# Moving a step-of-four layout from what TensorE reads to what it writes, in blockwise causal attention with a channel mix

## The chip, the cores and the metric

The kernel runs on one core of a Trainium2 chip. The metric is the time of one execution on the device in microseconds. The kernel before takes 314.23 us, the median of three runs (314.18 to 315.11); the profiled execution spans 312.8 us, with a mean granted TensorE clock of 0.989 of full speed.

## The reference

Eight batches with eight heads of 576 positions and 64 dimensions go through attention in which a query sees all keys of its own block of 64 positions and of earlier blocks. The heads' outputs, side by side, are the input of a channel mix with two matrix products and a gate.

```python
scores = scale * np.matmul(q, k.transpose(0, 1, 3, 2))        # 8 x 8 x 576 x 576
mask = block_i >= block_j                                      # blocks of 64
scores = np.where(mask, scores, -1000000000.0)
attn = np.exp(scores - np.max(scores, axis=-1, keepdims=True))
attn = attn / (np.sum(attn, axis=-1, keepdims=True) + 1e-09)
x = np.matmul(attn, v)                     # then (batch, position, head*dim): 8 x 576 x 512
...
xk = mu_k * x + (1.0 - mu_k) * x_prev      # x_prev: the position before
xr = mu_r * x + (1.0 - mu_r) * x_prev
k = np.maximum(xk @ w_k, 0.0)              # 512 -> 1024
v = k * k @ w_v                            # 1024 -> 512
out = v / (1.0 + np.exp(-(xr @ w_r)))
```

## The kernel before

The work is written as tasks of engines (PE is TensorE, DVE VectorE, ACT ScalarE, POOL GpSimd); a planner in the program puts them in a fixed order for each engine, and TensorE's order is a list of names (`s` scores, `d` and `e` sums, `v` value products, `k`, `r`, `p` the channel mix). Here are the constants, and the steps of attention that the change touches.

```python
P, D, S, CUT, J = 128, 64, 576, 512, 4
M = CUT // J                    # 128: 512 queries are 128 groups (p) of 4 classes (j)
RINGS = {..., "e": 4, "c": 2, "rd": 3, "s": 2, "mm": 4, ...}     # buffers of each kind; s, mm in PSUM
TURNED = 2                      # batches 0 and 1 are transposed on TensorE, 2 to 7 by DMA
```

In batches 0 and 1 the transposed queries (64 dimensions on partitions, queries along the free axis, bf16) lie in their natural order, query 4p + j at column 4p + j. In batches 2 to 7 they lie class by class, query 4p + j at column 128 j + p. The last 64 of the 576 queries are treated by themselves. The keys of a block of 128 are the stationary operand of a score; the two heads of a pair use the two halves of the array's rows. In the later batches one pair of heads has scores of 512, 384, 256 and 128 columns for the first 512 queries, and some of 64 for the last:

```python
LATER = [
    [(0, 0, 0, M)],                                    # (column, key block, groups from, to)
    [(0, 0, M, WD), (D, 1, 32, M), (448, 1, M, WD)],
    [(0, 2, H2, M), (256, 2, M, WD), (320, 3, 96, M), (448, 3, M, WD)],
]
...
if a < M:
    moving = ask[:, J * a:J * z]                       # L649 on: scores
    dst = PS[:, h, col:col + J * w]
    if b >= TURNED:
        moving = ask[:, 0:CUT].rearrange("d (j p) -> d p j", j=J)[:, a:z]
        dst = dst.rearrange("k (p j) -> k p j", j=J)
    nc.tensor.matmul(dst, keys, moving, start=True, stop=True)     # L657
else:
    nc.tensor.matmul(PS[:, h, col:col + D], keys, ask[:, CUT:S], ...)   # L660
```

So scores stand in natural query order in PSUM; in the later batches the moving operand is read with a hop of 128 elements at each element. ScalarE makes exponentials of 1024 of them at a time (two heads, L679), in fp16; GpSimd zeroes those of the first 64 queries of a block against its second 64 keys (L688):

```python
nc.scalar.activation(tiles["e", b, pr][:, :, i, :], tiles["ps", b, pr, i], AF.Exp, scale=ISQ)
...
nc.gpsimd.memset(tiles["e", b, pr][D:P, :, i, col:col + D], 0.0)
```

The sums and the value products use the array as four column tiles of 32, one for each of four heads, that work side by side (all at L721). The sums take one class at a time, so that the sums of class j land on row j of a head's rows; the value products take 32 of the 64 dimensions at a time:

```python
tiled(PS[:, lo - a:z - a], FOURTH[:, (J - j) % J:(J - j) % J + R],      # sums
      probs(b, 4 * Q + g, kc, lo, z)[:, j::J], g, ...)
...
ps = PS[:, cols]                                                        # values
if a < M:
    ps = ps[:, J * (lo - a):J * (z - a)]
tiled(ps, V[:, kc, 4 * Q + g, x:D:2], probs(b, 4 * Q + g, kc, lo, z), g, ...)
```

VectorE takes the reciprocals of the sums (L772, and L775 for the last 64 queries), spreads each class over all rows of its head with a shuffle, and multiplies:

```python
nc.vector.reciprocal(tiles["c", key][:, 0:z - a], PS[:, 0:z - a])       # L772
...
for j in range(J):
    nc.vector.stream_shuffle(tiles["rd", key][:, J * a + j:J * z:J],    # L781
                             tiles["c", key][:, 0:z - a], [j] * 32)
...
num = num[:, 0:n * J * (z - a)].rearrange("p (s t) -> p s t", s=n)[:, :, lo - first:hi - first]
r = r[:, lo - b * S:hi - b * S]
nc.vector.tensor_tensor(x, num, r.unsqueeze(1).to_broadcast([P, n, hi - lo]), ALU.mult)   # L825
```

For each batch but the first and each half of the heads there are one group of sums (`d`), two value products for the first 512 queries (`v` 0 and 1) and one for the last 64 (`v` 2); the first batch has the same columns in two groups.

Of the kernel before, what the change touches and what calls it, by code (L numbers as in the profile page):

```python
# [20 lines left out]
TURNED = 2  # L21
# [259 lines left out]
def kernel(  # L281
# [24 lines left out]
    M = CUT // J  # L306
    WD = M + D
    JT = S // D
    CH = 512
    CHUNKS = [(0, CH // 2), (CH // 2, CH // 2)] + [  # L310
        (i * CH, CH) for i in range(1, B * S // CH)]
# [303 lines left out]
    def add_score(b, pr, i):  # L615


        sbuf = plan.buf("s")
        tail = i is None
        Q = pr // 2  # L620
        takes, uses = [sbuf], [tiles["qktbuf", b]]
        if tail:
            takes.append(el_buf[b][Q])
            deps = sum([evac[x, b, pr + y] for x in ("qkt", "tail")
                        for y in range(2)], [])
            if b:
                deps.append(ready["l", b - 1, Q])
            mms = [(pr + x, x * D, J, M, WD) for x in range(2)]
        else:
            mms = [(pr,) + p for p in pieces(b)[i]]  # L630
            deps = evac["qkt", b, pr] + (
                evac["tail", b, pr] if any(p[3] == M for p in mms) else [])
            if i == 0:
                tiles["ebuf", b, pr] = plan.buf("e")
                takes.append(tiles["ebuf", b, pr])
            else:
                uses.append(tiles["ebuf", b, pr])

        def fn():
            qkt = tiles["qkt", b]  # L640
            PS = tiles["ps", b, pr, i] = new("s", [P, 2, 512], FP)
            if i == 0:
                tiles["e", b, pr] = new("e", [P, 2, 3, 512], F16)
            for p, col, kc, a, z in mms:
                for h in range(2):
                    rows = slice(h * D, h * D + D)
                    keys, ask = qkt[rows, p, 1], qkt[rows, p, 0]
                    w = z - a
                    keys = keys[:, kc * P:kc * P + P]  # L649
                    if a < M:  # L650
                        moving = ask[:, J * a:J * z]
                        dst = PS[:, h, col:col + J * w]
                        if b >= TURNED:
                            moving = ask[:, 0:CUT].rearrange(
                                "d (j p) -> d p j", j=J)[:, a:z]
                            dst = dst.rearrange("k (p j) -> k p j", j=J)
                        nc.tensor.matmul(dst, keys, moving, start=True,  # L657
                                         stop=True)
                    else:
                        nc.tensor.matmul(PS[:, h, col:col + D], keys,  # L660
                                         ask[:, CUT:S], start=True, stop=True)
        pe = on("PE", 0.06 if tail else 0.215 + 0.02 * i, fn, deps, takes, uses,
                name=f"s{b}t{Q}" if tail else f"s{b}{pr}{i}", mode="rows",
                steps=2 * len(mms))
        if tail:
            def exl():
                nc.scalar.activation(
                    E4s[b % 2][0:D, 4 * Q:4 * Q + 4].rearrange(
                        "p (h a) q -> p h a q" if b < TURNED else
                        "p (a h) q -> p h a q", h=2),  # L670
                    tiles["ps", b, pr, i][0:D, :, 0:2 * D].rearrange(
                        "p h (a q) -> p h a q", q=D), AF.Exp, scale=ISQ)
            ready["l", b, Q] = on("ACT", 0.27, exl, [pe],
                                  uses=[sbuf, el_buf[b][Q]])
            return
        ebuf = tiles["ebuf", b, pr]

        def ex():
            nc.scalar.activation(tiles["e", b, pr][:, :, i, :],  # L679
                                 tiles["ps", b, pr, i], AF.Exp, scale=ISQ)  # L680
        t = on("ACT", 0.905, ex, [pe] + ([ready["x", b, pr, 0]] if i else []),
               uses=[sbuf, ebuf])
        ready["x", b, pr, i] = t

        def zero():
            for col, kc, a, z in pieces(b)[i]:
                if a == kc * 32 and a < M:
                    nc.gpsimd.memset(  # L688
                        tiles["e", b, pr][D:P, :, i, col:col + D], 0.0)
        n = sum(a == kc * 32 and a < M for col, kc, a, z in pieces(b)[i])  # L690
        if n:
            ready["z", b, pr, i] = on("POOL", 0.15 * n, zero, [t], uses=[ebuf])

    def probs(b, head, kc, a, z):


        if kc == J:
            return E4s[b % 2][:, head]
        i, col, a0, z0 = [
            (i, col, a0, z0) for i, piece in enumerate(pieces(b))  # L700
            for col, k0, a0, z0 in piece if k0 == kc and a0 <= a and z <= z0][0]
        pr, h = place(b, head)
        E = tiles["e", b, pr][:, h, i, col:]
        if a == M:
            return E[:, 0:D]
        return E[:, J * (a - a0):J * (z - a0)]

    def add_values(b, Q):

# [14 lines left out]
        def sums(PS, a, z):  # L724
            kcs = [kc for kc in range(J) if kc * 32 < z]
            for j in range(J):
                for kc in kcs:
                    lo = max(a, kc * 32)
                    for g in range(G):
                        tiled(PS[:, lo - a:z - a],  # L730
                              FOURTH[:, (J - j) % J:(J - j) % J + R],
                              probs(b, 4 * Q + g, kc, lo, z)[:, j::J], g,
                              (j, kc) == (0, kcs[0]), (j, kc) == (J - 1, kcs[-1]))
            for kc in range(J + 1) if z == M else ():
                for g in range(G):
                    tiled(PS[:, M:WD], ONES, probs(b, 4 * Q + g, kc, M, WD), g,
                          kc == 0, kc == J)

        def part(PS, xs, a, z):
            V = VOs[b % 2]  # L740
            wide = J * (z - a) if a < M else D
            for n, x in enumerate(xs):
                cols = slice(n * wide, n * wide + wide)
                kcs = [kc for kc in range(J) if kc * 32 < z] + [J] * (a == M)
                for kc in kcs:
                    lo = max(a, kc * 32)
                    for g in range(G):
                        ps = PS[:, cols]
                        if a < M:
                            ps = ps[:, J * (lo - a):J * (z - a)]  # L750
                        tiled(ps, V[:, kc, 4 * Q + g, x:D:2],
                              probs(b, 4 * Q + g, kc, lo, z), g,
                              kc == kcs[0], kc == kcs[-1])

        def group(name, a, z, deps, steps, dur, r_dur, s_dur):
# [11 lines left out]

            def recip():
                tiles["c", key] = new("c", [P, M], FP)
                tiles["rd", key] = new("rd", [P, S], FP)  # L770
                PS = tiles["den", key]
                nc.vector.reciprocal(tiles["c", key][:, 0:z - a],  # L772
                                     PS[:, 0:z - a])
                if z == M:
                    nc.vector.reciprocal(tiles["rd", key][:, CUT:S],  # L775
                                         PS[:, M:WD])
            t = on("DVE", r_dur, recip, [t], takes=[cbuf, rd], uses=[dbuf])

            def spread():
                for j in range(J):  # L780
                    nc.vector.stream_shuffle(  # L781
                        tiles["rd", key][:, J * a + j:J * z:J],
                        tiles["c", key][:, 0:z - a], [j] * 32)
            return rd, on("DVE", s_dur, spread, [t], uses=[cbuf, rd]), key

# [20 lines left out]
        def scale(t, i, xs, a, z, c, first, lo, hi, buf, rd, spr, key):  # L806
# [5 lines left out]
            def norm():  # L812
                x = xt_tile(c)[:, ch, 1 + off:1 + off + hi - lo]
                num, r = tiles["num", b, Q, i], tiles["rd", key]
                n = len(xs)
                if a == M:
                    nc.vector.tensor_tensor(
                        x, num[:, 0:n * D].rearrange("p (s t) -> p s t", s=n),
                        r[:, CUT:S].unsqueeze(1).to_broadcast([P, n, D]),
                        ALU.mult)  # L820
                    return
                num = num[:, 0:n * J * (z - a)].rearrange(
                    "p (s t) -> p s t", s=n)[:, :, lo - first:hi - first]
                r = r[:, lo - b * S:hi - b * S]
                nc.vector.tensor_tensor(  # L825
                    x, num, r.unsqueeze(1).to_broadcast([P, n, hi - lo]),
                    ALU.mult)
            dur = 0.2 if a == M else 0.00105 * (hi - lo) * len(xs) + 0.065
            xb = xtbuf[home]
            n = on("DVE", dur, norm, [t, spr], takes=[xb] if take else [],  # L830
# [294 lines left out]
```

## Time and profile before

| | |
|---|---|
| time, median of 3 | 314.23 us |
| span of the profiled execution | 312.8 us |
| TensorE matmul busy | 294.1 us, 94% |
| VectorE busy | 220.5 us, 71% |
| ScalarE busy | 202.1 us, 65% |
| GpSimd busy | 114.1 us, 36% |
| scores of the first 512 queries (L657) | 272 matmuls, busy 71.2 us |
| exponentials (L679) | 96, mean 1024 ns |
| spreading of reciprocals (L781) | 72 shuffles, busy 42.8 us |
| normalisation (L825) | 60, busy 23.6 us |

A line of a group view names the line, engine and operation, the tiles (out<-in), partitions x elements and type, the count, the busy time and the mean of one instruction, and then the idle time of the engine before them with what ended it. In a timeline each row has the start, the time from the first start to the last end of the merged instructions, and their number (x). [...]In the chain of waits, shares belong to the chain of work that ended last.

### The profile page before, as it was taken

How to read it: one execution, taken by the hardware profiler on the slowest of the kernel's cores; microseconds unless marked ns; L12 is line 12 of the kernel's file. 1: busy time of each engine (PE TensorE's matmuls, PEld its weight loads, DVE VectorE, ACT ScalarE, POOL GpSimd, SP SyncE). 2: the span in 40 equal slices, each digit the busy share in tenths (PEclk: the TensorE clock that was granted, in tenths of full speed). 3: DMA queues.
4: the chain of work that ended last, by engine and by line, in shares of the span. 5: the costliest groups of instructions: out<-in, count | busy, mean ns of one | idle time of the engine just before them, and what ended most of it. 6: DMA issues, size and time to landing. Idle time of an engine off the chain costs nothing.

```text
span 312.8 us, 9964 instructions
## 1 busy us (share of the span) xinstructions
PE 294.1 (94%) x4120; PEld 139.5 (45%) x4120; DVE 220.5 (71%) x477; ACT 202.1 (65%) x313; POOL 114.1 (36%) x265
## 2 busy tenths in 40 slices
PE   1987799999999999899999999999999999999996
PEld 1664566344434345424344334443434354444443
DVE  3789999985198935991678817796587728999232
ACT  3868798868776678259761888538865766065360
POOL 3256559430431444343441574325451333000200
PEclk9998699999999999999999999999999999999999
DMA  7999979999999985893969339985942100020303
GB/s 259 308 262 246 245 229 242 256 227 227 263 200 205 234 195 105 190 256 82 206 131 254 126 68 208 188 234 131 173 85 72 69 2 2 34 103 0 137 0 134
DMA packets 118301, 51.51 MB, mean 165 GB/s; under 512 B 102768, under 2 KB 109168, under 8 KB 118256
## 3 DMA queue, kind: packets, MB, share of 16 engines
q1 hardware_dynamic: 118256, 50.88, 68.0%
q8 instruction: 32, 0.52, 0.7%
q14 instruction: 13, 0.11, 0.1%
HBM read 33.56 MB, written 9.44 MB: 137 GB/s over the span
## 4 chain that ended last, share of the span: by engine, by line
PE 80%; DVE 12%; ACT 4%; issue 2%; DMA 1%; SPq 0%; POOL 0%; DVEq 0%; ACTq 0%
PE t_mm L948 19%; PE t_s L657 17%; PE t_mm L1014 17%; PE t_mm L721 13%; PE t_mm L983 10%; DVE t_rd L781 5%; ACT t_e L679 3%; PE t_s L660 2%; DVE t_xt L825 2%; DMA t_ld<-in_q_dram 1%; PE t_mm L469 1%; DVE t_c L772 1%; DVE t_d L897 1%; DVE t_xk L910 1%; DVE t_rd L775 1%
## 5 line engine op out<-in xcount | busy, mean ns | idle before, releaser
L679 ACT ACTIVATE t_e<-t_s 128x1024 f16<-128x1024 f32 x96 | 95.1, 1024 | 53.6 <-PE t_s L660 26.6
L657 PE MATMUL t_s<-t_qkt 64*128 64x128 bf16 (+3 forms) x272 | 71.2, 588 | 1.5 <-ACT t_e L679 1.4
L948 PE MATMUL t_mm<-t_xk,WK 128*128 128x512 f16 (+1 forms) x320 | 69.1, 359 | 1.9 <-DVE t_xt L825 1.2
L1014 PE MATMUL t_mm<-WV,t_k 128*128 128x512 f16 (+1 forms) x296 | 66.1, 374 | 0.5 <-DVE t_o L1026 0.5
L688 POOL MEMSET t_e<- 64x128 f16 x128 | 24.0, 205 | 91.3 <-ACT t_e L679 89.6
L959 ACT ACTIVATE t_kr<-t_mm 128x512 f32<-128x512 f32 (+1 forms) x80 | 43.7, 560 | 18.5 <-PE t_mm L948 17.5
L948 PEld LDWEIGHTS <-WK 128*128 128x128 f16 x320 | 28.9, 98 | 38.7 <-issue 8.8
L1014 PEld LDWEIGHTS <-t_k 128*128 128x128 f16 x296 | 27.4, 98 | 38.4 <-issue 8.7
L772 DVE RECIPROCAL t_c<-t_mm 128x128 f32<-128x128 f32 (+1 forms) x18 | 15.6, 868 | 40.1 <-PE t_mm L721 40.0
L781 DVE STREAM_SHUFFLE t_rd<-t_c 128x128 f32<-128x128 f32 (+1 forms) x72 | 42.8, 868 | 0.0
L968 POOL TENSOR_TENSOR t_k<-t_kr 128x512 f16<-128x512 f32 (+1 forms) x27 | 26.1, 974 | 31.5 <-ACT t_kr L959 31.4
L983 PE MATMUL t_mm<-WR,t_xr 128*128 128x512 f16 x144 | 35.9, 380 | 0.0
L994 ACT ACTIVATE t_t<-t_mm 128x512 f32<-128x512 f32 x36 | 21.5, 600 | 20.5 <-PE t_mm L983 19.9
L968 DVE TENSOR_TENSOR t_k<-t_kr 128x512 f16<-128x512 f32 (+1 forms) x24 | 17.6, 743 | 23.1 <-ACT t_kr L959 23.1
L1026 DVE SCALAR_TENSOR_TENSOR t_o<-t_t,t_mm 128x512 f32<-128x512 f32 (+1 forms) x37 | 24.9, 681 | 12.5 <-PE t_mm L1014 9.6
L721 PE MATMUL t_mm<-t_e,VO 128*32 128x64 f16 (+4 forms) x1056 | 29.4, 251 | 2.1 <-DVE t_xt L825 1.0
L910 DVE SCALAR_TENSOR_TENSOR t_xk<-t_d,MUK,t_xt 128x512 f16<-128x512 f32 (+1 forms) x40 | 28.8, 747 | 1.7 <-POOL t_d L897 1.6
L910 DVE SCALAR_TENSOR_TENSOR t_xr<-t_d,MUR,t_xt 128x512 f16<-128x512 f32 (+1 forms) x40 | 29.8, 770 | 0.0
L660 PE MATMUL t_s<-t_qkt 64*128 64x64 bf16 x320 | 27.7, 204 | 1.1 <-ACT t_e L679 1.1
L825 DVE TENSOR_TENSOR t_xt<-t_mm,t_rd 128x448 f32<-128x448 f32 (+7 forms) x60 | 23.6, 436 | 4.1 <-PE t_mm L721 3.0
L657 PEld LDWEIGHTS <-t_qkt 64*128 64x128 bf16 x272 | 13.8, 101 | 27.5 <-issue 25.1
L721 PEld LDWEIGHTS <-VO 128*32 128x32 f16 x1184 | 19.4, 98 | 14.5 <-issue 6.5
(60 smaller groups left out, 291.0 us busy)
## 6 DMA issues: line engine op xcount, KB each, us to landing
out_dram<-t_o SPq DMA_DIRECT2D x35, 256.0 KB, 2.2
t_vl<-in_v_dram SPq DMA_DIRECT2D x32, 256.0 KB, 4.9
t_ld<-in_k_dram SPq DMA_DIRECT2D x48, 128.0 KB, 4.0
t_ld<-in_q_dram SPq DMA_DIRECT2D x24, 256.0 KB, 4.2
t_ld<-in_q_dram SPq DMA_DIRECT2D x8, 288.0 KB, 5.5
t_ld<-in_k_dram SPq DMA_DIRECT2D x8, 288.0 KB, 5.1
t_ld<-in_moe_w_k_dram SPq DMA_DIRECT2D x8, 256.0 KB, 5.0
t_ld<-in_moe_w_v_dram SPq DMA_DIRECT2D x8, 256.0 KB, 4.3
```

Source lines behind the costliest of these rows:

```text
L657: nc.tensor.matmul(dst, keys, moving, start=True, stop=True)
L660: nc.tensor.matmul(PS[:, h, col:col + D], keys, ask[:, CUT:S], start=True, stop=True)
L679: nc.scalar.activation(tiles["e", b, pr][:, :, i, :], tiles["ps", b, pr, i], AF.Exp, scale=ISQ)
L721: nc.tensor.matmul(ps[g * R:g * R + R], lhs, e, start=start, stop=stop, tile_position=(0, g * R))
L781: nc.vector.stream_shuffle(tiles["rd", key][:, J * a + j:J * z:J], tiles["c", key][:, 0:z - a], [j] * 32)
L825: nc.vector.tensor_tensor(x, num, r.unsqueeze(1).to_broadcast([P, n, hi - lo]), ALU.mult)
L910: nc.vector.scalar_tensor_tensor(tiles[name, h][:, cc, o:o + w], tiles["d", c, cc][:, 0:w], (MUK1, MUR1)[n][:, cc:cc + 1], xt_tile(c)[:, c ...
L948: nc.tensor.matmul(ps[:, 0:w], WK[:, cc, jc * P:(jc + 1) * P], tiles["xk", h][:, cc, o:o + w], start=(cc == 0), stop=(cc == CCn - 1))
L959: nc.scalar.activation(tiles["kr", c, jc][:, 0:w], tiles["pk", c, jc][:, 0:w], AF.Relu)
L968: (nc.vector if eng == "DVE" else nc.gpsimd).tensor_tensor(K2, KR, KR, ALU.mult)
L983: nc.tensor.matmul(ps, tiles["xr", h][:, cc, o + jt * P:o + (jt + 1) * P], WR[:, cc], start=(cc == 0), stop=(cc == CCn - 1))
L1014: nc.tensor.matmul(ps[:, 0:w], tiles["k2", h][:, jc, off:off + P], WV[:, jc, cols], start=(jc == 0), stop=(jc == JCn - 1))
```

## The change

The classes now stay apart from the scores to the exponentials: within one piece the queries stand class by class, so the scores of the later batches and the sums read and write runs of neighbouring elements. The natural order is restored where the value products write PSUM: they write every fourth column, one class after the other. The reciprocals of a class are kept together too, 129 columns from one class to the next, and the multiplication picks them from four places. In batches 0 and 1, whose queries lie in natural order, the scores now read with a step of four elements. The number of instructions, their order, the buffers and the waits are not touched.

```diff
+    MP = M + 1
@@ scores
-                        moving = ask[:, J * a:J * z]
-                        dst = PS[:, h, col:col + J * w]
-                        if b >= TURNED:
-                            moving = ask[:, 0:CUT].rearrange(
-                                "d (j p) -> d p j", j=J)[:, a:z]
-                            dst = dst.rearrange("k (p j) -> k p j", j=J)
-                        nc.tensor.matmul(dst, keys, moving, start=True,
-                                         stop=True)
+                        nc.tensor.matmul(
+                            PS[:, h, col:col + J * w].rearrange(
+                                "p (j n) -> p j n", j=J), keys,
+                            ask[:, 0:CUT].rearrange(
+                                "d (p j) -> d j p" if b < TURNED else
+                                "d (j p) -> d j p", j=J)[:, :, a:z],
+                            start=True, stop=True)
@@ zeroing
-                        tiles["e", b, pr][D:P, :, i, col:col + D], 0.0)
+                        tiles["e", b, pr][D:P, :, i, col:col + J * (
+                            z - a)].rearrange(
+                            "p h (j n) -> p h j n", j=J)[:, :, :, 0:D // J],
+                        0.0)
@@ exponentials as read by sums and values
-        return E[:, J * (a - a0):J * (z - a0)]
+        return E[:, 0:J * (z0 - a0)].rearrange("p (j n) -> p j n", j=J)[
+            :, :, a - a0:z - a0]
@@ sums
-                              probs(b, 4 * Q + g, kc, lo, z)[:, j::J], g,
+                              probs(b, 4 * Q + g, kc, lo, z)[:, j], g,
@@ values
-                            ps = ps[:, J * (lo - a):J * (z - a)]
+                            ps = ps.rearrange("q (n j) -> q j n", j=J)[
+                                :, :, lo - a:z - a]
@@ reciprocals, shuffles
-                tiles["rd", key] = new("rd", [P, S], FP)
+                tiles["rd", key] = new("rd", [P, J * MP + D], FP)
-                        tiles["rd", key][:, J * a + j:J * z:J],
+                        tiles["rd", key][:, j * MP + a:j * MP + z],
@@ normalisation
+                p0, p1 = (lo - b * S) // J, (hi - b * S) // J
                 num = num[:, 0:n * J * (z - a)].rearrange(
-                    "p (s t) -> p s t", s=n)[:, :, lo - first:hi - first]
-                r = r[:, lo - b * S:hi - b * S]
-                nc.vector.tensor_tensor(
-                    x, num, r.unsqueeze(1).to_broadcast([P, n, hi - lo]),
-                    ALU.mult)
+                    "q (s p j) -> q s p j", s=n, j=J)[:, :, p0 - a:p1 - a]
+                r = r[:, 0:J * MP].rearrange("q (j p) -> q p j", j=J)[:, p0:p1]
+                x = x.rearrange("q s (p j) -> q s p j", j=J)
+                if n == 1:
+                    nc.vector.tensor_tensor(x[:, 0], num[:, 0], r, ALU.mult)
+                else:
+                    nc.vector.tensor_tensor(
+                        x, num, r.unsqueeze(1).to_broadcast(
+                            [P, n, p1 - p0, J]), ALU.mult)
... (the last 64 queries' reciprocals move to the end of the wider tile)
```

More of the change, by code (lines that the diff above doesn't have):

```diff
@@ L774, in recip @@
                 if z == M:
-                    nc.vector.reciprocal(tiles["rd", key][:, CUT:S],
+                    nc.vector.reciprocal(tiles["rd", key][:, J * MP:],
                                          PS[:, M:WD])
@@ L818, in norm @@
                         x, num[:, 0:n * D].rearrange("p (s t) -> p s t", s=n),
-                        r[:, CUT:S].unsqueeze(1).to_broadcast([P, n, D]),
+                        r[:, J * MP:].unsqueeze(1).to_broadcast([P, n, D]),
                         ALU.mult)
                     return
+                p0, p1 = (lo - b * S) // J, (hi - b * S) // J
                 num = num[:, 0:n * J * (z - a)].rearrange(
-                    "p (s t) -> p s t", s=n)[:, :, lo - first:hi - first]
-                r = r[:, lo - b * S:hi - b * S]
-                nc.vector.tensor_tensor(
-                    x, num, r.unsqueeze(1).to_broadcast([P, n, hi - lo]),
-                    ALU.mult)
+                    "q (s p j) -> q s p j", s=n, j=J)[:, :, p0 - a:p1 - a]
[7 more added lines that the diff above has]
+                            [P, n, p1 - p0, J]), ALU.mult)
             dur = 0.2 if a == M else 0.00105 * (hi - lo) * len(xs) + 0.065
```

## The prediction

> **What bounds the kernel now.** I read the page from the top, first for the engine that is never idle and then for the stretch in which that holds.
>
> ```profile
> PE 294.1 (94%) x4120; PEld 139.5 (45%) x4120; DVE 220.5 (71%) x477; ACT 202.1 (65%) x313; POOL 114.1 (36%) x265
> ...
> PE 80%; DVE 12%; ACT 4%; issue 2%; DMA 1%; SPq 0%; POOL 0%; DVEq 0%; ACTq 0%
> PE t_mm L948 19%; PE t_s L657 17%; PE t_mm L1014 17%; PE t_mm L721 13%; PE t_mm L983 10%; DVE t_rd L781 5%; ACT t_e L679 3%; PE t_s L660 2%; DVE t_xt L825 2%; DMA t_ld<-in_q_dram 1%; PE t_mm L469 1%; DVE t_c L772 1%; DVE t_d L897 1%; DVE t_
> ```
>
> TensorE is the bound: 94% busy, 80% of the chain of waits. The three lines that the change touches on TensorE are L657 (scores, 17% of the chain), L721 (sums and value products, 13%) and, on VectorE, L781 (spreading the reciprocals, 5%) and L825 (normalisation, 2%). The windows view, cut where attention's first batches end and where the last one ends, says where TensorE has room:
>
> ```profile
> core 0: us, PE busy (x) PEld busy (x) DVE busy (x) ACT busy (x) POOL busy (x), PEclk, DMA share, GB/s
> 0.00:60.00 60.00, 47.47 (x1138) 32.80 (x1142) 49.88 (x130) 46.03 (x77) 33.30 (x79) 0.94 0.98 258
> 60.00:275.00 215.00, 211.94 (x2823) 90.30 (x2815) 150.10 (x315) 138.32 (x205) 78.60 (x184) 1.00 0.69 154
> 275.00:313.00 38.00, 34.72 (x168) 16.36 (x168) 20.56 (x34) 17.77 (x32) 2.25 (x3) 0.99 0.21 77
> ```
>
> Before 60 us no engine is full, and VectorE (49.9 of 60) is busiest; from 60 to 275 us TensorE has 3 us free of 215, while VectorE is at 70% and ScalarE at 64%; after 275 us there is no attention. What the change saves on TensorE is therefore worth most in the middle stretch.
>
> How long single operations occupy TensorE I read from start to start in its timeline, since the duration of one matmul also holds its latency:
>
> ```profile
> 94.84 1.02 PE L657 MATMUL t_s<-t_qkt 64*128 64x512 bf16 x2
> 95.80 1.36 PE L721 MATMUL t_mm<-t_e,FOURTH 128*32 128x128 f16 x64
> 96.98 0.30 PE L721 MATMUL t_mm<-t_e,ONES 128*32 128x64 f16 x16
> 97.10 0.20 PE L721 MATMUL t_mm<-EL,ONES 128*32 128x64 f16 x4
> 97.24 0.20 PE L660 MATMUL t_s<-t_qkt 64*128 64x64 bf16 x2
> 97.28 0.81 PE L657 MATMUL t_s<-t_qkt 64*128 64x384 bf16 x2
> 97.91 0.21 PE L660 MATMUL t_s<-t_qkt 64*128 64x64 bf16 x2
> 97.96 0.59 PE L657 MATMUL t_s<-t_qkt 64*128 64x256 bf16 x2
> 98.38 0.21 PE L660 MATMUL t_s<-t_qkt 64*128 64x64 bf16 x2
> 98.43 0.38 PE L657 MATMUL t_s<-t_qkt 64*128 64x128 bf16 x2
> 98.63 0.21 PE L660 MATMUL t_s<-t_qkt 64*128 64x64 bf16 x2
> 98.77 0.73 PE L721 MATMUL t_mm<-t_e,VO 128*32 128x512 f16 x16
> 99.43 1.02 PE L657 MATMUL t_s<-t_qkt 64*128 64x512 bf16 x2
> ```
>
> A pair of scores 384 wide holds the engine 97.91 - 97.28 = 0.63 us, 256 wide 0.42, 128 wide 0.20: 1.64 ns a column. The sixteen value matmuls (four column tiles side by side, 512 + 384 + 256 + 128 = 1280 columns) take 99.43 - 98.77 = 0.66 us with a change of mode, and the chain of waits has runs of eight full matmuls of 512 in 1.73 us, 0.42 ns a column. So the scores of these batches run at a quarter of the rate. The 64 sum matmuls (four classes of 320 columns, 1280 in all) take 96.98 - 95.80 = 1.18 us, 0.92 ns a column.
>
> **What the Trainium skill says.** "TensorE: Matmul & The Clock Gate", section "Back-to-back issue gap", gives a warm matmul N/2.4 + 2.5 ns; the trace agrees (0.216 us at 512). "Advanced Engine Details and Errata", section "Memory Cachelines", says that SBUF has lines of 16 bytes and needs two hits on a line for full rate. The trace bears out the penalty: scores that hop 256 bytes at each 2-byte element pay four times. It doesn't quite bear out the "two hits": sums that step 8 bytes, two elements to a line, still run at about half rate. "PSUM — Partial Sum Buffer", section "Specifications (TRN2)", says that PSUM's lines are 8 bytes and that "any non-contiguous AP slows matmuls significantly", without a number; nothing in the kernel before writes PSUM with a step, so no row shows the size. "Vector Engine (DVE) Microarchitecture Reference", section "5.2 Measured stream behaviour on trn2", lists 1.05 ns a column for contiguous words, 1.73 where one source hops at every element, 2.5 for small steps. Here the normalisation is contiguous and has 1.04 ns a column ((613 - 281) / (448 - 128) from the groups by form); the shuffle, which writes with a step of 16 bytes, is far worse, as follows.
>
> ```profile
> 126.22 1.00 DVE L781 STREAM_SHUFFLE t_rd<-t_c 128x128 f32<-128x128 f32 x1
> ...
> 126.85 1.00 DVE L781 STREAM_SHUFFLE t_rd<-t_c 128x128 f32<-128x128 f32 x1
> ```
>
> They start 0.62 us apart; those 64 wide start 0.34 apart (31.52, 31.86, 32.20). The slope is (0.62 - 0.34)/64 = 4.4 ns a column, the fixed part 0.06 us.
>
> **The change, part by part.** Instructions, their order, buffers and waits stay; only patterns change, so each item is a number of columns by a new rate.
>
> Scores, batches 2 to 7 (24 pairs of heads): a pair of heads has 1280 such columns, now 0.84 (1.02 less the 0.18 of latency that the 384 wide row shows) + 0.63 + 0.42 + 0.20 = 2.09 us. They read contiguous runs after the change: 1280 x 0.42 = 0.54 us. Saved: 1.55 x 24 = 37 us.
>
> Scores, batches 0 and 1 (8 pairs): now contiguous, then a step of 8 bytes. Charged with about the rate of the sums, 0.4 ns a column more: 1280 x 8 x 0.4 = +4 us.
>
> Sums (16 groups of 1280 columns): contiguous afterwards. Widths 128 and 96 at 0.42 ns, widths 64 and 32 at the 0.03 us that a set of four takes in the rows with ONES (sixteen from 96.98 to 97.10): 0.056 + 0.042 + 0.03 + 0.03 = 0.16 a class, 0.63 a group against 1.18. Saved: 0.55 x 16 = 9 us.
>
> Value products (16 groups, two of 1280 columns each): 40960 columns, 17 us at 0.42. They will write every fourth fp32 word, so each column has an 8-byte line to itself where now two share one. My estimate from the PSUM page is half the rate: +17 us. This is the doubtful term.
>
> TensorE in all: -37 + 4 - 9 + 17 = -25 us, of which the middle stretch (24 pairs, 12 groups) has -37 - 6.6 + 12.8 = -31, and the first 60 us +4 - 2.2 + 4.3 = +6.
>
> VectorE: shuffles written contiguously, estimated at the 1.04 ns of the normalisation over the same fixed 0.06: 0.20 us instead of 0.62 at 128 wide, 0.13 instead of 0.34 at 64. 56 x 0.42 + 16 x 0.21 = -27 us. The normalisation reads the reciprocals with a hop of 129 words at each element; 16 x 1024 columns x (1.73 - 1.04), the first from the page, is an estimate of +11 us. Net -16 us on an engine that is not the bound, but each group's way from sums to normalised values becomes about 1 us shorter. The zeroing on GpSimd (24 us busy) gets shorter runs; I charge nothing.
>
> From engine time to kernel time: in the middle stretch TensorE would need 181 us, VectorE about 150 - 18 + 8 = 140 and ScalarE 138. No engine overtakes TensorE, but matmuls are in a fixed order with two score buffers, and an exponential takes 1.02 us: where scores follow each other closely TensorE, now held 0.65 us by its own scores, will wait for ScalarE. I take three quarters of the saving, -23 us. In the first 60 us TensorE gains 6 us of work but has 12.5 us idle, and VectorE, the busiest, sheds some 4: zero net. 314.2 - 23 = 291 us.
>
> **Rivals.** First, the step in PSUM costs four times rather than twice, like the hops in SBUF: value products +51 us instead of +17, TensorE +9, and with the shorter VectorE chain 314 to 320 us. For it speaks the fourfold price of hopping reads here; against it, that a PSUM line holds only two words, so at most one word is lost. Second, the step costs nothing: TensorE -42 us, about 281. Third, ScalarE takes over as the bound: score waits on the exponentials eat half of the saving, about 299. For it speaks that ScalarE shows 8 or 9 tenths in a third of the middle slices; against it, its mean of 64%. Fourth, the normalisation at 129 words costs the page's 2.5 ns: VectorE +24 instead of +11, nearly what the shuffles save, and 2 or 3 us on the whole.
>
> **Range and chances.** I give the doubled price 55%, a free step 15%, three or four times 25%, worse 5%. These lie at 291, 281, 302 to 318, and above 325. The range 279 to 316 holds the first two and half of the third. Faster by over 2% (below 307.9) then has 0.79, within 2% 0.12, slower 0.09.
>
> **What would show it.** Scores L657 of 512 columns with a duration near 0.4 instead of 1.02 us and 17% of the chain falling to about 5%; sums near 0.65 us from start to start; value products of sixteen taking about 1.1 us (2.1 under the first rival, 0.55 under the second); shuffles about 0.2 us apart; the normalisation of 448 columns near 0.9 us; the exponentials named as releasers of L657 with tens of microseconds if the third rival holds. A value product above 2 us would make the prediction wrong.

## The result, and the profile after

The changed kernel takes 281.82 us (median of four runs, 279.33 to 283.02) against 314.31: a ratio of 0.8951, 95% interval 0.8888 to 0.9015. That is 33.0 us less (0.1049 x 314.3). It lies within the stated range and below the predicted 291.

First the page of the kernel after: the shares of the engines, and the chain of waits by engine and by line. The lines have moved: L652 is the scores, L725 the sums and value products, L786 the shuffles, L833 and L835 the normalisation; L958, L993 and L1024 are the channel mix.

```profile
PE 265.9 (95%) x4120; PEld 134.8 (48%) x4120; DVE 204.0 (73%) x477; ACT 197.0 (70%) x313; POOL 113.2 (40%) x265
...
PE 82%; DVE 7%; ACT 5%; issue 2%; DMA 2%; POOL 0%; SPq 0%; DVEq 0%
PE t_mm L958 22%; PE t_mm L725 18%; PE t_mm L1024 18%; PE t_mm L993 11%; PE t_s L652 7%; ACT t_e L679 3%; PE t_s L660 3%; DMA t_ld<-in_k_dram 2%; DVE t_xt L833 1%; PE t_mm L470 1%; DVE t_d L907 1%; DVE t_o L1036 1%; DVE t_xk L920 1%; ACT t_
```

TensorE is still the bound, with 28.2 us less of work. The scores have gone from 17% of the chain to 7%, the sums and value products together from 13% to 18%, and the shuffles from 5% to under 1% (1.8 us). The windows view, cut again at the first batches and at the end of attention (now near 250 us), shows the middle stretch as full as before, and shorter:

```profile
0.00:60.00 60.00, 49.29 (x1080) 31.68 (x1082) 44.00 (x130) 44.54 (x74) 34.04 (x78) 0.97 0.95 248
60.00:250.00 190.00, 188.50 (x2907) 89.79 (x2902) 145.96 (x327) 139.74 (x218) 77.11 (x186) 1.00 0.87 182
```

TensorE has 1.5 us free of 190 there. Now TensorE's timeline over one stretch, to be read from start to start:

```profile
82.23 0.39 PE L652 MATMUL t_s<-t_qkt 64*128 64x512 bf16 x2
82.55 0.79 PE L725 MATMUL t_mm<-t_e,FOURTH 128*32 128x128 f16 x64
83.18 0.29 PE L725 MATMUL t_mm<-t_e,ONES 128*32 128x64 f16 x16
...
85.91 1.26 PE L725 MATMUL t_mm<-t_e,VO 128*32 128x512 f16 x16
87.10 0.28 PE L652 MATMUL t_s<-t_qkt 64*128 64x256 bf16 x2
```

A pair of scores 512 wide leaves the engine after 0.32 us, with the change of mode; the 64 sums take 83.18 - 82.55 = 0.63 us instead of 1.18; the sixteen value matmuls 87.10 - 85.91 = 1.19 us instead of 0.66. On VectorE the shuffles and the normalisation, as rows of its timeline:

```profile
84.87 0.30 DVE L786 STREAM_SHUFFLE t_rd<-t_c 128x128 f32<-128x128 f32 x1
...
85.08 0.30 DVE L786 STREAM_SHUFFLE t_rd<-t_c 128x128 f32<-128x128 f32 x1
...
87.22 0.82 DVE L833 TENSOR_TENSOR t_xt<-t_mm,t_rd 128x384 f32<-128x384 f32 x1 [0.51 <-PE t_mm L725]
```

The shuffles start 0.21 us apart instead of 0.62.

Adding up by what each matmul moves the end of TensorE's work onward, over the whole trace: scores of the first 512 queries 62.5 us before and 27.2 after, sums 21.6 and 11.8, value products 25.8 and 43.8. That is -35.3, -9.8 and +18.0, -27.1 in all; the other 1.1 us of the 28.2 lie in lines that the change doesn't touch. By the same account TensorE stood idle for 9.2 us between its first and its last matmul before, and for 5.1 after: the span less its busy time, less the time to the first matmul (6.4 and 7.1 us) and less the 3.1 us after the last.

### The profile page after: what moved, and what is told of

Read it like the earlier page. It is cut to its first block, busy times and chain, and to the rows that moved or that the text cites. A ratio compares the mean times of both kernels' runs of the same rounds, so it can differ in the third digit from the quotient of the medians.

```text
span 281.2 us, 9965 instructions
## 1 busy us (share of the span) xinstructions
PE 265.9 (95%) x4120; PEld 134.8 (48%) x4120; DVE 204.0 (73%) x477; ACT 197.0 (70%) x313; POOL 113.2 (40%) x265
## 4 chain that ended last, share of the span: by engine, by line
PE 82%; DVE 7%; ACT 5%; issue 2%; DMA 2%; POOL 0%; SPq 0%; DVEq 0%
PE t_mm L958 22%; PE t_mm L725 18%; PE t_mm L1024 18%; PE t_mm L993 11%; PE t_s L652 7%; ACT t_e L679 3%; PE t_s L660 3%; DMA t_ld<-in_k_dram 2%; DVE t_xt L833 1%; PE t_mm L470 1%; DVE t_d L907 1%; DVE t_o L1036 1%; DVE t_xk L920 1%; ACT t_qkt L392 1%; PE t_mm L1062 1%
## 5 line engine op out<-in xcount | busy, mean ns | idle before, releaser
L958 PE MATMUL t_mm<-t_xk,WK 128*128 128x512 f16 (+1 forms) x320 | 68.9, 358 | 1.3 <-ACT t_kr L969 0.5
L1024 PE MATMUL t_mm<-WV,t_k 128*128 128x512 f16 (+1 forms) x296 | 66.0, 374 | 0.0
L725 PE MATMUL t_mm<-t_e,VO 128*32 128x64 f16 (+4 forms) x1056 | 47.4, 340 | 0.8 <-issue 0.6
L958 PEld LDWEIGHTS <-WK 128*128 128x128 f16 x320 | 29.2, 98 | 32.0 <-issue 3.7
L1024 PEld LDWEIGHTS <-t_k 128*128 128x128 f16 x296 | 27.4, 98 | 32.3 <-issue 2.9
L978 POOL TENSOR_TENSOR t_k<-t_kr 128x512 f16<-128x512 f32 (+1 forms) x27 | 27.1, 1010 | 29.4 <-ACT t_kr L969 29.2
L833 DVE TENSOR_TENSOR t_xt<-t_mm,t_rd 128x448 f32<-128x448 f32 (+6 forms) x56 | 30.8, 593 | 9.5 <-PE t_mm L725 9.1
L652 PE MATMUL t_s<-t_qkt 64*128 64x128 bf16 (+3 forms) x272 | 35.9, 326 | 1.8 <-ACT t_e L679 1.4
L993 PE MATMUL t_mm<-WR,t_xr 128*128 128x512 f16 x144 | 35.9, 380 | 0.0
L725 PEld LDWEIGHTS <-VO 128*32 128x32 f16 x1184 | 24.0, 112 | 21.2 <-issue 18.3
L1036 DVE SCALAR_TENSOR_TENSOR t_o<-t_t,t_mm 128x512 f32<-128x512 f32 (+1 forms) x37 | 24.3, 666 | 10.9 <-PE t_mm L1024 8.6
L978 DVE TENSOR_TENSOR t_k<-t_kr 128x512 f16<-128x512 f32 (+1 forms) x24 | 16.5, 699 | 18.8 <-ACT t_kr L969 18.7
L920 DVE SCALAR_TENSOR_TENSOR t_xr<-t_d,MUR,t_xt 128x512 f16<-128x512 f32 (+1 forms) x40 | 29.5, 763 | 0.0
L660 PE MATMUL t_s<-t_qkt 64*128 64x64 bf16 x320 | 23.7, 196 | 0.4 <-ACT t_e L679 0.3
L907 POOL TENSOR_TENSOR t_d<-t_xt 128x512 f32<-128x512 f32 (+1 forms) x17 | 16.4, 966 | 14.6 <-DVE t_xt L833 11.3
L993 PEld LDWEIGHTS <-t_xr 128*128 128x128 f16 x144 | 13.4, 98 | 16.2 <-issue 0.5
```

Source lines behind the costliest of these rows:

```text
L652: nc.tensor.matmul(PS[:, h, col:col + J * w].rearrange("p (j n) -> p j n", j=J), keys, ask[:, 0:CUT].rearrange("d (p j) -> d j p" if b < T ...
L725: nc.tensor.matmul(ps[g * R:g * R + R], lhs, e, start=start, stop=stop, tile_position=(0, g * R))
L833: nc.vector.tensor_tensor(x[:, 0], num[:, 0], r, ALU.mult)
L920: nc.vector.scalar_tensor_tensor(tiles[name, h][:, cc, o:o + w], tiles["d", c, cc][:, 0:w], (MUK1, MUR1)[n][:, cc:cc + 1], xt_tile(c)[:, c ...
L958: nc.tensor.matmul(ps[:, 0:w], WK[:, cc, jc * P:(jc + 1) * P], tiles["xk", h][:, cc, o:o + w], start=(cc == 0), stop=(cc == CCn - 1))
L978: (nc.vector if eng == "DVE" else nc.gpsimd).tensor_tensor(K2, KR, KR, ALU.mult)
```

## The experiments

Four of them (x1, x2, x3, x10) make one part of the change alone in the kernel before; x5 joins two parts, and the rest undo or vary a part of the changed kernel. Each ratio is to the kernel before on the same chip, and microseconds gained are what the ratio lacks of 1, times 314.3. "TensorE work" and "TensorE idle" are read from one trace of each kernel, counted as above. The work also moves with the granted clock: x3 leaves TensorE's instructions as they were and has 2.6 us less of it, in a trace with a granted clock of 0.999 against 0.989 before. So differences of 2 or 3 us in that column can't be put down to an edit. The time of x8 is the median of three runs; a fourth, of 273.79 us, was in a slower state.

| kernel | time, us | ratio, 95% interval | TensorE work | TensorE idle |
|---|---|---|---|---|
| before | 314.3 | | 294.1 | 9.2 |
| x1: contiguous scores alone | 286.88 | 0.9095 (0.9056 to 0.9134) | 255.1 | 18.9 |
| x2: step of four in PSUM alone | 326.95 | 1.0367 (1.0318 to 1.0416) | 308.8 | 5.4 |
| x3: VectorE's part alone | 310.27 | 0.9836 (0.9797 to 0.9875) | 291.5 | 6.3 |
| x10: contiguous sums alone | 308.85 | 0.9799 (0.9759 to 0.9839) | 286.6 | 10.9 |
| x5: x1 and x3 together | 276.09 | 0.8770 (0.8742 to 0.8799) | 254.8 | 11.1 |
| changed kernel | 281.82 | 0.8951 (0.8888 to 0.9015) | 265.9 | 5.1 |
| x6: changed, VectorE's part undone | 286.32 | 0.9094 (0.9080 to 0.9107) | 266.4 | 8.3 |
| x7: changed, classes 128 apart | 280.28 | 0.8900 (0.8885 to 0.8915) | 264.7 | 5.6 |
| x9: changed, first batches contiguous | 280.87 | 0.8905 (0.8880 to 0.8930) | 262.8 | 6.6 |
| x8: changed, PSUM written in pairs | 272.00 | 0.8620 (0.8568 to 0.8673) | 249.6 | 11.6 |
| x11: x8, VectorE's part undone | 280.08 | 0.8897 (0.8858 to 0.8936) | 250.7 | 16.6 |
| x4: changed, PSUM contiguous, VectorE restores the order | 271.11 | 0.8587 (0.8544 to 0.8631) | 251.8 | 8.0 |

**x1, the scores alone.**

```diff
-                                "d (j p) -> d p j", j=J)[:, a:z]
-                            dst = dst.rearrange("k (p j) -> k p j", j=J)
+                                "d (j p) -> d j p", j=J)[:, :, a:z]
+                            dst = dst.rearrange("k (j p) -> k j p", j=J)
```

> The kernel before with one edit: in batches 2 to 7 the scores read each class as a contiguous run and write it as one; nothing else follows, so the queries of these batches come out in another order and the zeroing hits other elements. Theory A (every microsecond taken from TensorE's own work is a microsecond of time): TensorE's scores fall by about 37 us, time 275 to 280 us. Theory B (the prediction's three quarters: TensorE then waits for exponentials, and the shorter VectorE work made up for it in the whole change): time 285 to 290 us, with at least 8 us more of TensorE idle.

TensorE lost 39.0 us and the kernel 28.4: 0.73 of it. TensorE's idle doubled. But the waits of TensorE in x1 name another engine than the expectation (engine, line waited for; us in total, times, longest). First those of the kernel before, then those of x1:

```profile
PE t_s L657 <- ACT t_e L679: 1.4, 3, 0.6
PE t_mm L948 <- DVE t_xt L825: 1.2, 2, 0.7
PE t_s L660 <- ACT t_e L679: 1.1, 2, 0.8
PE t_mm L721 <- DVE t_xt L825: 1.0, 1, 1.0
```

```profile
PE t_mm L948 <- DVE t_xt L825: 5.1, 4, 1.7
PE t_mm L721 <- DVE t_xt L825: 2.1, 3, 1.0
PE t_mm L1014 <- DVE t_xt L825: 1.9, 2, 1.4
PE t_s L657 <- ACT t_e L679: 1.7, 4, 0.7
...
PE t_s L660 <- ACT t_e L679: 1.3, 2, 1.0
```

Compare 9.1 us of waiting for the normalisation (L825), 2.2 in the rows before, with 3.0 us for exponentials, 2.5 before. Theory B has the right time and the wrong cause. None of the waiting products reads normalised values: L721 reads exponentials, L948 the mixed inputs, L1014 squares of the first product. But they all write one of the four PSUM buffers that `RINGS` calls `mm`, and the normalisation reads the value products there. So what TensorE waits for is a buffer that VectorE has yet to empty. No run changes the number of these buffers.

**x2, the step in PSUM alone.**

```diff
-                            ps = ps[:, J * (lo - a):J * (z - a)]
+                            ps = ps.rearrange("q (n j) -> q j n", j=J)[
+                                :, :, lo - a:z - a]
... (the exponentials are read as four runs, one after the other)
```

> The kernel before with one edit: the value products write every fourth column of PSUM, class after class, from exponentials in natural order; the values come out in another order. Both theories: value products 18 us dearer on TensorE. Theory A: time 330 to 334 us. Theory B (part of it hides in waits): 324 to 329 us.

Plus 11.5 us (10.0 to 13.1 by the interval) for 14.7 us of TensorE work, 0.78 of it, as theory B has it; TensorE's idle falls from 9.2 to 5.4 us. Value products cost 42.3 us of TensorE here and 43.8 in the changed kernel, so the price belongs to the step and not to the rest of the change.

**x3, VectorE's part alone.** The edit is the part of the change from the reciprocals to the normalisation.

> The kernel before with VectorE's part of the change alone: shuffles write a class contiguously, 129 columns apart, and the normalisation picks from four places; the result is the same. TensorE is not touched. Theory A: only idle time of TensorE on VectorE's chain can go, some 4 us: 309 to 312 us. Theory B needs 6 us or more from here: 308 us or less.

5.2 us less by the ratio, which is theory A's range; the interval, 3.9 to 6.4 us, still touches theory B's 6. In this kernel TensorE has nearly all its old work, and VectorE's shorter chain finds little waiting to remove: its idle falls from 9.2 to 6.3 us.

**x10, the sums alone.**

```diff
-                              probs(b, 4 * Q + g, kc, lo, z)[:, j::J], g,
+                              probs(b, 4 * Q + g, kc, lo, z)[
+                                  :, j * (z - lo):(j + 1) * (z - lo)], g,
```

> The kernel before with one edit: the sums of a class read a contiguous quarter of each run of exponentials instead of every fourth element, so a class sums other queries than its own. TensorE's sums fall by 9.8 us. Theory A (one for one): 304 to 307 us. Theory B (three quarters): 307 to 309 us.

6.3 us, in theory B's range, but the interval, 5.1 to 7.6 us, reaches into theory A's. The sums themselves fell by 8.9 us; TensorE's work as a whole by 7.5, and the first product of the channel mix was 1.8 us dearer in this trace, which has a granted clock of 0.66 from 170 to 175 us.

The four parts alone make -28.4 + 11.5 - 5.2 - 6.3 = -28.4 us. The whole is -33.0, so 4.6 us come from parts working together, with an uncertainty of about 3 us from the five intervals. The first batches' dearer scores are not among the four.

**x5, scores and VectorE's part together.** The edits are those of x1 and x3.

> The kernel before with contiguous scores (batches 2 to 7, as in x1_scores) and VectorE's part of the change together (as in x3_vector); the exponentials again stand in another order than sums and products take them. Theory C (once scores are fast, TensorE waits for normalised values, and VectorE's shorter chain takes that wait away): TensorE's idle falls from 18.9 us to 11 or less and time to 275 to 280 us, so VectorE's part is worth 7 us or more here, against 4.6 alone. Theory D (the part is worth the same everywhere, the idle has another cause): 282 to 284 us with idle of 14 us or more.

Minus 38.7 us, where the two alone make 33.6: 5.1 us more, with an uncertainty of about 2, and about as much as the sum above lacked. The VectorE part is worth 10.3 us beside fast scores (38.7 - 28.4) and about 5 without them. TensorE's waits in x5 show what went, and what came next:

```profile
PE t_s L658 <- DMA t_qkt<-NB: 2.5, 1, 2.5
PE t_s L658 <- ACT t_e L680: 1.8, 3, 0.9
PE t_mm L954 <- DVE t_xt L829: 1.4, 3, 0.7
```

The waits for the normalisation fell from 9.1 us to 1.4 in these rows; a transposing DMA has one wait of 2.5 us. Theory C holds for this pair (its idle of "11 or less" came out as 11.1), with the word that TensorE waits for the buffers of the values and not for the values.

**x6 and x11, VectorE's part undone.** The edit puts the old shuffles and the old normalisation into the changed kernel (x6) and into the faster kernel x8 (x11).

> The changed kernel with VectorE's part undone: shuffles write with a step of four, the normalisation reads contiguously; the result is the same. Theory C: 288 to 293 us, TensorE's idle up from 5.1 to 11 us or more, named as waits on the normalisation. Theory D: 285 to 287 us, idle 8 to 10.

4.5 us more, 8.3 us idle: theory D's range, not C's. The changed kernel's own interval is wide (2 us either way); against x7 below, which does the same work, it is 6.1 us. TensorE's waits for the normalisation, in the changed kernel and in x6:

```profile
PE t_mm L958 <- DVE t_xt L833: 0.3, 1, 0.3
```

```profile
PE t_mm L953 <- DVE t_xt L830: 2.7, 4, 1.3
...
PE t_mm L725 <- DVE t_xt L830: 0.5, 1, 0.5
```

With the step in PSUM TensorE has 266 us of work, and the old chain of VectorE holds it up by only 3 us more than the new. So I asked whether TensorE's pace decides:

> The changed kernel with value products in pairs (as in x8_pairs) and VectorE's part undone (as in x6_no_vector); the values come out in another order. TensorE has about 250 us of work. Theory E (what VectorE's part is worth depends on TensorE's pace: with 266 us of work it hid most of the old chain, with 250 it can't): 282 us or more, ten or more above x8_pairs, idle 19 us or more. Theory F (the part is worth some 4.5 us in the changed layout at any pace, and the 10.8 us next to fast scores had to do with the old layout): 275 to 279 us, idle 13 to 16.

The result lies between the two: 8.7 us above x8 by the ratios (0.8897 - 0.8620), idle 16.6. The waits of TensorE in x11 are again for the normalisation:

```profile
PE t_mm L954 <- DVE t_xt L831: 5.1, 4, 1.7
PE t_mm L1020 <- DVE t_xt L831: 2.5, 2, 1.7
PE t_mm L725 <- DVE t_xt L831: 2.5, 3, 1.0
```

and those of x8 partly for something else:

```profile
PE t_s L652 <- DMA t_qkt<-NB: 2.9, 1, 2.9
PE t_mm L959 <- DVE t_xt L834: 2.6, 3, 1.2
```

VectorE's part takes 10.1 us of such waits down to 2.6, and a wait for a DMA of 2.9 us takes the place of some of it. So its worth rises as TensorE gets faster, in the new layout from 4.5 (or 6.1) to 8.7 us, a little less than theory E said. The intervals leave 2 us of uncertainty either way on the 8.7 and about as much on the 10.3 beside fast scores in the old layout, so no difference between the layouts is shown.

**x7, the distance of 129.** One line, `MP = M` instead of `MP = M + 1`.

> The changed kernel with the classes of reciprocals 128 columns apart instead of 129; the result is the same. If the distance is only a matter of hopping: normalisation of 448 columns stays at 0.93 us and time at 281 to 283 us. If classes 128 columns apart get in each other's way, it takes 1.4 us or more, VectorE has 8 us or more of extra work, and time is 284 to 288 us.

The group by form of the normalisation, first of the changed kernel, then of x7:

```profile
L833 DVE TENSOR_TENSOR t_xt<-t_mm,t_rd 128x448 f32<-128x448 f32 x8 | 7.4, 929 | 2.5 <-PE t_mm L725 2.4
```

```profile
L833 DVE TENSOR_TENSOR t_xt<-t_mm,t_rd 128x448 f32<-128x448 f32 x8 | 7.4, 930 | 2.6 <-PE t_mm L725 2.4
```

929 and 930 ns, and intervals that overlap: the odd distance does nothing here. The time of 280.28 us lies 0.7 us below the first range.

**x8, pairs in PSUM.**

```diff
-                            ps = ps.rearrange("q (n j) -> q j n", j=J)[
-                                :, :, lo - a:z - a]
+                            ps = ps.rearrange("q (n u t) -> q u n t", u=2, t=2)[
+                                :, :, lo - a:z - a]
```

> The changed kernel, but the value products write PSUM as pairs of neighbouring columns with a step of four between pairs, so that the values come out in another order. If what costs is that a column has an 8-byte line to itself, pairs are as cheap as contiguous columns: value products 26 us of TensorE instead of 44, time 263 to 272 us. If any step costs, they stay at 40 us or more and time at 280 to 283 us.

The value products of 512 columns by form, in the changed kernel and in x8:

```profile
L725 PE MATMUL t_mm<-t_e,VO 128*32 128x512 f16 x112 | 17.5, 611 | 0.0
```

```profile
L725 PE MATMUL t_mm<-t_e,VO 128*32 128x512 f16 x112 | 11.3, 385 | 0.0
```

385 ns is what they took before the change, and TensorE's share for all value products is 25.6 us, against 25.8 before. The pairs step as the single columns did, so what costs is the single column, as lines of two words have it. The time ends at the upper edge of the expected range, with idle up to 11.6 us.

**x9, the first batches.**

```diff
-                                "d (p j) -> d j p" if b < TURNED else
-                                "d (j p) -> d j p", j=J)[:, :, a:z],
+                                "d (j p) -> d j p", j=J)[:, :, a:z],
```

> The changed kernel, but batches 0 and 1 read their queries as contiguous runs too, as if they lay class by class, so that these batches' scores are taken for other queries than meant. TensorE loses the 3.6 us by which the step of 8 bytes made the first batches' scores dearer. If the first 60 us have room on TensorE, as the prediction took it: 281 to 283 us, unchanged. If a microsecond of TensorE's work is a microsecond there too: 277 to 279 us.

TensorE's scores fell by 3.4 us; the time by 1.4 us by the ratios (0.8951 - 0.8905), with about 2 us of uncertainty, so neither reading is ruled out. The traces say a part: the first scores of batch 2 start at 59.67 us in the changed kernel and at 58.25 in x9, 1.4 us earlier, with 3.1 us less of TensorE's work before them.

**x4, the order restored by VectorE.** The changed kernel, but the value products write PSUM class after class, and the normalisation picks both operands from four places:

```diff
-                            ps = ps.rearrange("q (n j) -> q j n", j=J)[
+                            ps = ps.rearrange("q (j n) -> q j n", j=J)[
@@ normalisation
-                    "q (s p j) -> q s p j", s=n, j=J)[:, :, p0 - a:p1 - a]
+                    "q (s j p) -> q s p j", s=n, j=J)[:, :, p0 - a:p1 - a]
```

> The changed kernel, but the value products write PSUM contiguously, class after class, and VectorE's normalisation reads both its operands from four places, so that it alone restores the order; the result is the same. TensorE loses the 18 us of the step. If reading PSUM with a hop costs VectorE no more than the reciprocals' hop does already (about 1.75 ns a column): 262 to 267 us. If the two hops add up (2.4 ns a column or more): VectorE gets 11 us or more of work and time is 268 to 276 us.

271.11 us, the lowest time of the table (not to be told from x8's), and here the values are in their natural order: 11.4 us below the changed kernel by the ratios, whose intervals are apart. The normalisation of 448 columns in x4:

```profile
L833 DVE TENSOR_TENSOR t_xt<-t_mm,t_rd 128x448 f32<-128x448 f32 x8 | 7.4, 930 | 1.5 <-PE t_mm L725 1.4
```

930 ns again: once the reciprocals are read with a hop, reading PSUM with one too costs nothing more. The hop was free, as the first reading said, and yet the time is in the range of the second: value products lost 17.9 us, but TensorE's idle rose from 5.1 to 8.0 us and its busy time fell by only 14.1. Of what is missing, 1.9 us lie in the first product of the channel mix (67.4 us against 65.5); x4's trace has a granted clock of 0.58 from 97 to 101 us. TensorE's longest waits after the start are now these:

```profile
PE t_s L652 <- DMA t_qkt<-NB: 2.2, 2, 1.9
PE t_mm L958 <- DVE t_xt L833: 1.9, 3, 1.2
```

From 60 to 240 us TensorE still has only 4.7 us free of 180:

```profile
60.00:240.00 180.00, 175.31 (x2828) 85.39 (x2827) 143.53 (x324) 138.07 (x214) 79.36 (x182) 0.99 0.96 189
```

So TensorE remains the bound of x4. Whether the transposing DMA would be the next one, no run tests.

## Why the prediction was right, and where it was off

**Costs on TensorE: right.** Scores of the later batches -37 predicted, -38.9 in x1 (62.5 to 23.6); the first batches' step of 8 bytes +4, measured 3.6 (27.2 against 23.6); sums -9, measured -9.8, at 0.63 us a group as computed; value products +17, measured +18.0. In sum -27.1 instead of -25.

**The doubtful term: right, and its reason borne out.** The step in PSUM doubles the price of a column. The first rival (four times, 2.1 us for sixteen) and the second (free) fall by the 1.19 us of the timeline. The line of 8 bytes, which the Trainium skill's "PSUM — Partial Sum Buffer" states in "Specifications (TRN2)", agrees with x8: pairs of columns with the same step cost what contiguous columns do. Its "any non-contiguous AP slows matmuls significantly" does not: the pairs are not contiguous, and took 385 ns like the contiguous columns. That the line has 8 bytes and not, say, 16 of which two words must be hit, x8 can't tell.

**Costs on VectorE: right.** Shuffles 0.21 us apart (0.20 predicted), the normalisation 1.75 ns a column ((929 - 368) / (448 - 128), by form) against 1.73 in the section that the prediction cites. Net -16 us predicted, 16.5 measured (220.5 to 204.0). The -18 us of the shuffles in the middle stretch should read -20 by the prediction's own numbers (48 shuffles at 0.42); nothing hangs on it. The fourth rival, 2.5 ns, falls.

**From engine time to kernel time: the step that failed.** "I take three quarters of the saving, -23 us" should have been -33. Three quarters is what the scores give alone (0.73 in x1), but not what the whole change gives, not even with VectorE's part undone: x6 has 27.7 us less of TensorE's work than the kernel before and is 28.5 us faster. The traces show it for the stretch that the prediction meant, from the first score of batch 2 to the end of the span:

| kernel | starts at, us | length, us | TensorE busy, us | against before: work, length |
|---|---|---|---|---|
| before | 57.57 | 255.2 | 249.1 | |
| x1: contiguous scores alone | 58.74 | 225.8 | 211.1 | -38.0, -29.5 |
| x6: changed, VectorE's part undone | 59.36 | 225.7 | 217.5 | -31.6, -29.6 |
| changed kernel | 59.67 | 221.6 | 217.0 | -32.1, -33.7 |
| x11: value products in pairs, VectorE's part undone | 56.21 | 221.1 | 204.7 | -44.4, -34.1 |

The granted clock of these stretches was 1.00 in all five, and the work saved in the changed kernel was as predicted (31 us). Of the ten us by which -23 was short, about four are VectorE's shorter chain, for which I gave nothing; the other six are the lost quarter, which didn't appear: even with the old chain 0.94 of the saving came out as time. It does appear with the old chain where TensorE has less work left: 0.78 of the saving in x1, 0.77 in x11, where the value products are cheap again. There it is made by waits for PSUM buffers that the normalisation empties. The wait I named for it, scores waiting for exponentials, hardly grew (3.0 us in x1, 2.5 before) and is 1.7 us in the changed kernel. So the third rival, which needs tens of microseconds of it, falls too.

**The first 60 us, counted as zero: nearly.** The first score of batch 2 starts 2.1 us later in the changed kernel than before, and 0.8 us later in x7; the trace before has the lower granted clock there (0.83 from 20 to 40 us, 0.91 after), so the cost may be somewhat larger. Of the first batches' dearer scores x9 shows that a part reaches the time.

## What to carry to other kernels

When a layout has to be turned somewhere, price the turn in each place that could do it, in nanoseconds a column, and put it where an engine has time: here 1.64 where TensorE read its moving operand with a hop, twice the contiguous price where it wrote PSUM with a step, and nothing more on a VectorE read that hopped already. And before taking a share off a saving for waits, ask which engine frees what the faster one will wait for: if the same change shortens that engine's chain, the two gains can add up to more than they bring alone (x5), and the more so the faster the bound has become (x6 against x11).

## What the runs showed of the hardware

A shuffle that writes fp32 words with a step of 16 bytes costs 4.4 ns a column; written contiguously, 128 columns take 0.21 us from start to start instead of 0.62. The Trainium skill's "Vector Engine (DVE) Microarchitecture Reference", section "5.2 Measured stream behaviour on trn2", has 2.5 ns as its dearest row, so this step is worse than any listed there. Two hopping reads cost VectorE no more than one (930 against 929 ns for 448 columns), with one of them from PSUM. For TensorE, a step of 8 bytes in a 2-byte moving operand still costs 0.35 ns a column more than a contiguous read (3.6 us over 10240 columns), which bears out the prediction's doubt about two elements to a line.
